# Attention with a gated feed-forward layer: the causal masks of the float32 heads by GpSimd's selection, and the second head's decay row from SBUF on ScalarE's queue

## Chip, cores and metric

One core of a Trainium2 chip runs the whole program. The metric is the device time of one execution in microseconds (us); before the change the median of three runs is 1150.61 us (1149.22 to 1154.78).

The engines are TensorE (PE), VectorE (DVE), ScalarE (ACT), GpSimd (POOL) and SyncE (SP). DMA transfers are issued from the queues of SP, ACT and POOL, which the profile calls SPq, ACTq and POOLq. Each engine works off its own instructions in a fixed order and waits for others by semaphores.

## What is computed

Sixty-four attention heads (8 batches of 8) of 576 rows and 64 columns, with a decay bias made of a running sum, and then a gated layer over the 4608 rows of 512 columns that the heads give:

```python
scores = scale * np.matmul(q, k.transpose(0, 1, 3, 2))
causal = np.triu(np.ones((S, S), dtype=bool), k=1)
cum = np.cumsum(np.maximum(s, 0.0), axis=-1)
bias = -(cum[:, :, :, None] - cum[:, :, None, :])
scores = np.where(causal, -1000000000.0, scores + np.minimum(bias, 0.0))
scores = scores - np.max(scores, axis=-1, keepdims=True)
attn = np.exp(scores)
attn = attn / (np.sum(attn, axis=-1, keepdims=True) + 1e-09)
attn_out = np.matmul(attn, v)
# x: attn_out as 4608 rows of 512
gate = 1.0 / (1.0 + np.exp(-(x @ w_gate)))
out = (gate * (x @ w_val)) @ w_out
```

## The kernel before

**Heads and tiles.** The heads run one after another. Each head is cut into five tiles of query rows, taken from the largest (tile 4, 576 key columns) to the smallest (tile 0, 64 columns). Three kinds of heads follow each other. The first eight, the float32 heads (the first batch, `i < NN` in the code), keep q and k in float32, because the scales with which the others are split into float16 pairs are not there yet. Heads 9 to 16 (the second batch, `NN <= i < MK`) use float16 pairs. So do the rest.

**A float32 head.** `n_prep` (L599) turns q and k of two heads by PE (L614), and ACT copies them to SBUF (L618 to L621, the last being the key copy). `n_s` (L625) makes the scores of one tile in PSUM: one or two float32 products (L631), and then, for the block on the diagonal, one more product by `mask_scores` (L514, the product is L518) that adds 1e30 above the diagonal: a bfloat16 unit matrix `eye` times a constant matrix `above`. `n_max` (L635) is one DVE instruction (L643) that adds the head's decay row to the scores, writes them to SBUF and keeps each row's minimum (scores are held with their sign turned); its second part reads the minimum out. ACT takes the exponential (L644). `n_turn` (L646) turns the result by PE (L653) and ACT (L654), and `n_av` (L656) multiplies it by v (L662).

**The decay row.** `rel` (L166) holds the decay of all heads, one head in each partition. It is written to `cum_d` in HBM (L167). `load_crow` (L444) brings the row of head `i` from there into partition 0 of the tile `cr`, from SP's queue (L447); the first head needs no load, since its row is already in partition 0 of `rel`. `spread_crow` (L449) copies that row to all 128 partitions by POOL (L451). There are two `cr` tiles, so the load for head `i + 2` waits until head `i` no longer reads its tile. Float32 heads read `cr` itself (`bias_row`, L495); later ones read a scaled copy `rl`.

**Masks of the later heads.** In the second batch `s_part` (L481) adds the same bfloat16 product (L518) to its two float16 products (L489, L491). From head 17 on, `mask_part` (L507) does without it: POOL's `affine_select` (L511) writes 1e30 into the columns above the diagonal of `rl`, tile by tile, before `max_part` (L520, DVE L529) adds that row.

**Beside the heads.** During the first heads the kernel also loads the weights of the gated layer, decodes them from 64-bit numbers (ACT L298, DVE L299 to L301), takes a bound for each (PE L310, DVE L313) and splits them into float16 pairs (ACT L337, DVE L338). Their loads are on SP's queue for the first two (L284) and on ACT's queue for the others (L286). Squares of v are loaded from POOL's queue (L184). Each finished batch feeds the gated layer: PE products L714, tanh on ACT (L719), DVE L721, ACT L729 and DVE L730, and the output products L744.

**What sets the order.** The code is written tick by tick, one tile of one head each (L799). A scheduler then lays out each engine's instructions by its own estimate of durations; `tc.high_priority` (the helper `first`) raises the float32 heads in it. A change anywhere in the first heads so moves instructions of other kinds as well. DMA transfers share a small set of completion semaphores (named DMAHW0 to DMAHW7 in the order for the queues of SP and ACT): a transfer that takes a semaphore waits on its own queue until the earlier transfer with that semaphore has landed.

## Time and profile before

| | |
|---|---|
| median of three runs | 1150.61 us |
| the profiled execution, its own time | 1150.28 us |
| its span in the profile | 1148.5 us |
| PE busy | 1096.8 us (96%) |
| DVE busy | 756.4 us (66%) |
| ACT busy | 733.5 us (64%) |
| POOL busy | 199.9 us (17%) |
| first tile of head 2, start of DVE's L643 | 23.46 us |
| first tile of head 3 | 37.24 us |
| first tile of head 9 (DVE's L529) | 97.94 us |

The profile shows one execution. Start times are counted from the start of the span. A busy time is the time in which an engine had at least one instruction under way; products on PE overlap, so the recorded length of one is longer than the step from one to the next. In a row, a bracket names how long the engine had been idle before the instruction and what ended that time. The times of POOL are rough. A share of 96% on PE is a mean over the program: most of what is missing lies in its first fifth.

### The profile page before, as it was taken

How to read it: one execution, taken by the hardware profiler on the slowest of the kernel's cores; microseconds unless marked ns; L12 is line 12 of the kernel's file. 1: busy time of each engine (PE TensorE's matmuls, PEld its weight loads, DVE VectorE, ACT ScalarE, POOL GpSimd, SP SyncE). 2: the span in 40 equal slices, each digit the busy share in tenths (PEclk: the TensorE clock that was granted, in tenths of full speed). 3: DMA queues.
4: the chain of work that ended last, by engine and by line, in shares of the span. 5: the costliest groups of instructions: out<-in, count | busy, mean ns of one | idle time of the engine just before them, and what ended most of it. 6: DMA issues, size and time to landing. Idle time of an engine off the chain costs nothing.

```text
span 1148.5 us, 30266 instructions
## 1 busy us (share of the span) xinstructions
PE 1096.8 (96%) x11868; PEld 861.6 (75%) x11868; DVE 756.4 (66%) x2212; ACT 733.5 (64%) x1437; POOL 199.9 (17%) x473
## 2 busy tenths in 40 slices
PE   6998878999999999999999999999999999999998
PEld 4776757757777887788777777778877787787775
DVE  6868989876787777665565667777777775222222
ACT  5869667867776777676665667778676765233222
POOL 3301101022232222121211122212221211000000
PEclk9999999999999999999999999999999999999999
DMA  9766986997989688866645488878787774000000
GB/s 282 218 189 140 181 178 144 174 200 154 178 159 187 150 186 158 154 139 135 148 87 130 90 175 163 170 144 175 152 159 146 142 123 88 13 20 20 1 19 19
DMA packets 445517, 157.63 MB, mean 137 GB/s; under 512 B 403583, under 2 KB 435839, under 8 KB 445374
## 3 DMA queue, kind: packets, MB, share of 16 engines
q1 hardware_dynamic: 418686, 127.38, 56.7%
q10 hardware_dynamic: 23328, 17.04, 4.9%
q0 software_dynamic: 3360, 11.27, 2.8%
q8 instruction: 93, 1.52, 0.6%
q14 instruction: 50, 0.41, 0.1%
HBM read 56.92 MB, written 9.58 MB: 58 GB/s over the span
## 4 chain that ended last, share of the span: by engine, by line
PE 72%; DMA 10%; DVE 6%; issue 5%; ACT 3%; SPq 3%; POOL 1%; ACTq 0%; DVEq 0%; POOLq 0%
PE gv L714 39%; PE o L744 21%; DMA v<-in_v_dram 3%; PE s L491 3%; PE s L489 2%; DMA T<-qk 2%; PE na_ps L662 1%; SPq L463 1%; DVE e L529 1%; PE av L564 1%; PE av L562 1%; PE av L563 1%; DMA qk<-in_q_dram 1%; DMA w2all<-in_moe_w_out_dram 1%; PE s L631 1%
## 5 line engine op out<-in xcount | busy, mean ns | idle before, releaser
L714 PE MATMUL gv<-x,w 128*128 128x256 f16 (+3 forms) x6912 | 619.2, 247 | 10.1 <-DVE t2f L721 9.1
L714 PEld LDWEIGHTS <-w 128*128 128x128 f16 x6912 | 536.0, 98 | 75.0 <-issue 11.5
L744 PE MATMUL o<-w2all,h 128*128 128x512 f16 x1296 | 313.7, 379 | 1.8 <-ACT h L729 1.8
L530 ACT ACTIVATE e<-e,em 128x576 f32<-128x576 f32 x280 | 153.2, 556 | 92.5 <-DVE em L529 89.8
L744 PEld LDWEIGHTS <-h 128*128 128x128 f16 x1296 | 123.3, 98 | 109.1 <-ACT h L729 2.1
L719 ACT ACTIVATE th<-gv,scb 128x256 f32<-128x256 f32 (+3 forms) x288 | 110.8, 410 | 138.6 <-PE gv L714 130.5
L721 DVE SCALAR_TENSOR_TENSOR t<-th,gv 128x256 f32<-128x256 f32 x192 | 80.0, 417 | 147.9 <-ACT th L719 146.8
L511 POOL TENSOR_SCALAR_AFFINE_SELECT rl<-rl 128x128 f32<-128x128 f32 (+1 forms) x240 | 85.8, 358 | 503.1 <-DVE em L529 462.3
L529 DVE CUSTOM_DVE_ANT_0 e<-s,rl,qkcf 128x576 f32<-128x576 f32 x280 | 151.5, 545 | 31.7 <-PE s L491 15.6
L729 ACT ACTIVATE h<-t,hsc 128x256 f16<-128x256 f32 x192 | 96.7, 504 | 92.4 <-DVE t L721 92.4
L539 DVE SCALAR_TENSOR_TENSOR p<-e,p 128x384 f16<-128x384 f32 x224 | 103.1, 500 | 45.1 <-ACT p L534 44.3
L730 DVE SCALAR_TENSOR_TENSOR h<-t,hsc,h 128x256 f16<-128x256 f32 x192 | 93.7, 488 | 44.9 <-ACT h L729 42.6
L534 ACT ACTIVATE p<-e 128x1152 f16<-128x1152 f32 x112 | 111.9, 1000 | 2.7
L489 PE MATMUL s<-T 128*128 128x288 f16 (+2 forms) x246 | 64.1, 278 | 7.8 <-DVE em L529 4.0
L562 PE MATMUL av<-v,pt 128*128 128x65 f16 x560 | 67.7, 193 | 2.2 <-DMA pt<-p 2.2
L451 POOL PARTITION_BROADCAST cr<-cr x63 | 59.4, 947 | 56.0 <-DMA cr<-cum_d 42.0
L563 PE MATMUL av<-v,pt 128*128 128x64 f16 x560 | 67.7, 192 | 0.0
L564 PE MATMUL av<-v,pt 128*128 128x65 f16 x560 | 67.6, 194 | 0.0
L491 PE MATMUL s<-T 128*128 128x288 f16 (+2 forms) x246 | 61.5, 277 | 4.0 <-DMA T<-T 3.9
L562 PEld LDWEIGHTS <-pt 128*128 128x128 f16 x560 | 52.5, 97 | 7.9 <-DMA pt<-p 3.1
L563 PEld LDWEIGHTS <-pt 128*128 128x128 f16 x560 | 52.5, 97 | 4.5
L564 PEld LDWEIGHTS <-pt 128*128 128x128 f16 x560 | 52.7, 97 | 0.2
(164 smaller groups left out, 1297.0 us busy)
## 6 DMA issues: line engine op xcount, KB each, us to landing
v<-v SPq DMA_DIRECT2D x56, 162.5 KB
out_dram<-io POOLq DMA_DIRECT2D x34, 256.0 KB, 3.2
v<-in_v_dram SPq DMA_DIRECT2D x64, 128.0 KB
T<-T SPq DMA_DIRECT2D x82, 72.0 KB
t2f<-in_v_dram SPq DMA_DIRECT2D x20, 288.0 KB
qk<-in_q_dram SPq DMA_DIRECT2D x17, 288.0 KB
qk<-in_k_dram SPq DMA_DIRECT2D x17, 288.0 KB
w2all<-in_moe_w_gate_dram ACTq DMA_DIRECT2D x7, 512.0 KB
```

Source lines behind the costliest of these rows:

```text
L491: nc.tensor.matmul(ps[:, : b_ - a], lhs, T[i][:, 2, a:b_], start=False, stop=not mask)
L529: nc.vector.tensor_tensor_reduce(e, ps, r, c, MASKED, ALU.add, ALU.min, acc)
L530: nc.scalar.activation(e_t[t][:, :w], e_t[t][:, :w], AF.Exp, bias=acc, scale=-1.0)
L534: nc.scalar.activation(p_s[h_][:, 0], e_s[h_], AF.Copy, scale=PSCALE)
L539: nc.vector.scalar_tensor_tensor(flat[:, LOW[t] * P : (LOW[t] + t) * P], e_t[t][:, : t * P], PSCALE, flat[:, kb * P : (kb + t) * P], ALU.m ...
L562: nc.tensor.matmul(AV[i][:, t], hi, v_[:, D : 2 * D + 1], start=kb == 0, stop=False)
L563: nc.tensor.matmul(AV[i][:, t, 0:D], hi, v_[:, 0:D], start=False, stop=False)
L564: nc.tensor.matmul(AV[i][:, t], lo, v_[:, D : 2 * D + 1], start=False, stop=False)
L714: nc.tensor.matmul(ps[:, gv, a:e], w1[f][:, cc, gv, wl], x_of(b, cc)[:, xl, c0 + a : c0 + e], start=(c == 0), stop=(c == 3 * NC - 1))
L719: nc.scalar.activation(th[:, a:e], ps[:, 0, a:e], AF.Tanh, scale=scb[b][:, f : f + 1])
L729: nc.scalar.activation(h[:, 0], t2, AF.Copy, scale=hsc[:, f : f + 1])
L744: nc.tensor.matmul(ps[:m], h[:, hl, tt * P : tt * P + m], w2[f][:, wl], start=(f == 0 and c == 0), stop=(f == NF - 1 and c == 2))
```

## The change

Three things are changed, and the second batch keeps the bfloat16 product that it has.

- The float32 heads no longer call `mask_scores`. Instead `mask_part` has POOL select in their decay row `cr` itself, tile by tile, as the later heads have it done in `rl`. Tile `t` is selected only after DVE has read the row for the tile before it, since the same columns still counted there.
- The second head's row is no longer read back from HBM on SP's queue, but copied from partition 1 of `rel` to partition 0 of its `cr` tile by a DMA on ACT's queue. `tc.issue_after` places it behind the key copy of the first two heads, the last one noted in `kcopy`.
- `mask_scores` is now called for the second batch alone, and its start column is simplified.

```diff
 def load_crow(i):
     crow[i] = wp.tile([P, S], F32, tag="cr", name=f"cr{i}")
-    if i > 0:
+    if i == 1:
+        with tc.issue_after(kcopy[-1].ins):
+            nc.scalar.dma_start(crow[i][0:1], rel[1:2])
+    elif i > 1:
         nc.sync.dma_start(crow[i][0:1], cum_d[i : i + 1, :])
...
-            mask = i < MK and b_ == w
+            mask = NN <= i < MK and b_ == w
...
 def mask_part(i, t):
-    if i >= MK:
+    if i < NN or i >= MK:
         q0, m, w = TILES[t]
         nc.gpsimd.affine_select(rl[i][:, q0:w], rl[i][:, q0:w], pattern=[[-1, m]], compare_op=ALU.is_ge,
-                                fill=MASKED, base=m - P, channel_multiplier=1)
+                                fill=MASKED, base=0 if i < NN else m - P, channel_multiplier=1)
 def mask_scores(i, t, ps, a):
     q0, m, w = TILES[t]
-    c0 = 0 if i < NN else P - m
-    nc.tensor.matmul(ps[:, q0 - a : w - a], eye, above[:, c0 : c0 + m], start=False, stop=True)
+    nc.tensor.matmul(ps[:, q0 - a : w - a], eye, above[:, P - m :], start=False, stop=True)
...
-                    nc.scalar.copy(kt[:, cols], ps[:, :w])
+                    kcopy.append(nc.scalar.copy(kt[:, cols], ps[:, :w]))
...
-            nc.tensor.matmul(ps[:, : b_ - a], qT[i][:, q0 : q0 + P], kT[p][:, a:b_], start=True, stop=b_ < w)
-            if b_ == w:
-                mask_scores(i, t, ps, a)
+            nc.tensor.matmul(ps[:, : b_ - a], qT[i][:, q0 : q0 + P], kT[p][:, a:b_], start=True, stop=True)
```

Three places show how the instructions move. In the changed program the lines of `load_crow` to `mask_part` stand three further down: the broadcast is L454, the selection L514, the memset of v L462 to L464; those of `n_prep` stand two further down.

POOL at the start, before the change, from the first head's broadcast to behind the second head's (`cr_157` is the first head's row, `cr_196` the second's, `vsq` a load of v to be squared, `nq` a q tile of the third head that is set to zero):

```order
L451 ISA cr_157<-rel 128x576
L184 DMA vsq_0_263<-in_v_dram 128x576
L184 DMA vsq_1_277<-in_v_dram 128x576
L608 MEMSET nq_0_634 64x576
L184 DMA vsq_2_295<-in_v_dram 128x576
L451 ISA cr_196<-cr_196 128x576
L184 DMA vsq_3_319<-in_v_dram 128x576
```

The same place on POOL after the change, where the second head's row is `cr_195`:

```order
L454 ISA cr_157<-rel 128x576
L462 MEMSET v_1_257 64x130
L184 DMA vsq_0_264<-in_v_dram 128x576
L464 MEMSET v_0_159 128x10
L514 AFFINE_SELECT cr_157<-cr_157 128x128
L464 MEMSET v_1_257 128x10
L514 AFFINE_SELECT cr_157<-cr_157 128x128 x2
L610 MEMSET nq_0_667 64x576
L514 AFFINE_SELECT cr_157<-cr_157 128x128
L454 ISA cr_195<-cr_195 128x576
L184 DMA vsq_1_280<-in_v_dram 128x576
L514 AFFINE_SELECT cr_195<-cr_195 128x128
```

The second head's broadcast now stands behind four of the first head's five selections and ahead of two of the loads that it stood behind.

ACT around the first key copies, before the change, with the semaphores that each instruction waits for (`nk` is the turned k of the first two heads, `wa` and `ws` the first weight, `e_80` the scores of the large tiles):

```order
L621 COPY nk_167<-nq_ps_1_0_182 128x288 [waits PE_49]
L621 COPY nk_167<-nq_ps_1_1_187 128x288 [waits PE_49]
L298 ACTIVATE wa_147<-ws_146 128x1024 [waits DMAHW6_49,DMAHW5_49]
L644 ACTIVATE e_80<-e_80,em_4_248 128x576 [waits DVE_49]
L298 ACTIVATE w2all<-w2all 128x1024 [waits DMAHW7_49,DMAHW1_49]
L644 ACTIVATE e_80<-e_80,em_3_274 128x448 [waits DVE_49]
```

The same on ACT after the change:

```order
L623 COPY nk_167<-nq_ps_1_0_182 128x288 [waits PE_49]
L623 COPY nk_167<-nq_ps_1_1_187 128x288 [waits PE_49]
L448 DMA cr_195<-rel 1x16x36 [waits DMAHW5_49,DVE_49]
L298 ACTIVATE wa_147<-ws_146 128x1024 [waits DMAHW6_49]
L644 ACTIVATE e_80<-e_80,em_4_249 128x576 [waits DVE_49]
L644 ACTIVATE e_80<-e_80,em_3_277 128x448 [waits DVE_49]
L298 ACTIVATE w2all<-w2all 128x1024 [waits DMAHW7_49,DMAHW1_49]
```

The load of the second head's row waits for the semaphore of one half of the first weight (DMAHW5), for which the decode behind it waited before; the second decode has moved behind the exponential of the second tile.

DVE at the second head, before the change, from the split of the first weight on (`em_4` and `em_3` are the row minima of tiles 4 and 3, each followed by its read-out, which has one column):

```order
L338 SCALAR_TENSOR_TENSOR w_0_66<-wa_147,wscale,w_0_66 128x8x128
L334 TENSOR_SCALAR wscale<-xe_w_228 128x1
L643 ISA e_80,em_4_353<-s_4_322,cr_196 128x576
L643 ISA em_4_353 128x1
L643 ISA e_80,em_3_364<-s_3_345,cr_196 128x448
L643 ISA em_3_364 128x1
L338 SCALAR_TENSOR_TENSOR w_1_67<-w2all,wscale,w_1_67 128x8x128
```

The same on DVE after the change, down to the third tile:

```order
L338 SCALAR_TENSOR_TENSOR w_0_66<-wa_147,wscale,w_0_66 128x8x128
L643 ISA e_80,em_4_364<-s_4_329,cr_195 128x576
L643 ISA em_4_364 128x1
L313 TENSOR_SCALAR wj_238,wtot_237<-wps_228 128x128
L332 TENSOR_SCALAR xe_w_227<-wtot_237 128x1
L643 ISA e_80,em_3_377<-s_3_354,cr_195 128x448
L643 ISA em_3_377 128x1
L334 TENSOR_SCALAR wscale<-xe_w_227 128x1
L643 ISA e_79,em_2_432<-s_2_367,cr_195 128x320
```

The split of the first weight still stands ahead of the head's first tile; the bound of the second weight has moved in between its tiles, and the split of the second weight behind them.

More of the change, by code (lines that the diff above doesn't have):

```diff
@@ L379, in ffn_scale @@
             out_scale(b)
-    spreads = []
+    spreads, kcopy = [], []
     qk32, qkc, T, crow, v32, v16, vx, PT, xq, rl, AV = {}, {}, {}, {}, {}, {}, {}, {}, {}, {}, {}
```

## The prediction

> **What bounds the kernel now.** I read the page's 40 slices first, to see where TensorE (PE) is not full, then busy times by stretch (columns: stretch in us, length, busy us and instructions of PE, weight loads, VectorE (DVE), ScalarE (ACT) and GpSimd (POOL), granted clock, DMA share, GB/s).
>
> ```profile
> span 1148.5 us, 30266 instructions
> PE   6998878999999999999999999999999999999998
> DVE  6868989876787777665565667777777775222222
> 0.00:106.00 106.00, 89.63 (x661) 73.80 (x662) 74.26 (x213) 80.21 (x162) 26.58 (x62) 0.97 0.78 215
> 106.00:200.00 94.00, 72.96 (x797) 60.69 (x795) 88.45 (x238) 66.69 (x108) 10.40 (x12) 0.95 0.80 162
> 200.00:1148.50 948.50, 934.25 (x10417) 727.09 (x10414) 593.66 (x1763) 586.56 (x1168) 162.94 (x399) 1.00 0.62 126
> ```
>
> From 200 us on PE is busy 934.25 of 948.50 us: that part has its length whatever happens elsewhere, and only starts earlier or later. PE's idle time lies ahead of it: 106.00 - 89.63 = 16.4 us in the first stretch, 94.00 - 72.96 = 21.0 us in the second, where DVE is the full engine (88.45 of 94.00). The change touches the float32 heads, which lie in the first stretch. So the question is by how many microseconds those heads end earlier or later, and whether the DVE-bound stretch passes that on. Within the first stretch:
>
> ```profile
> 20.00:25.00 5.00, 3.29 (x31) 2.97 (x29) 2.78 (x8) 2.49 (x5) 0.86 (x1) 1.00 1.04 331
> 25.00:30.00 5.00, 3.85 (x15) 3.27 (x16) 1.63 (x3) 4.78 (x9) 0.55 (x1) 0.56 1.03 334
> 37.00:98.00 61.00, 55.13 (x427) 45.57 (x426) 43.66 (x135) 49.32 (x105) 11.88 (x22) 1.00 0.70 202
> ```
>
> Around 20 to 30 us every engine waits: DVE is idle for 2.22 + 3.37 = 5.6 us, PE runs at a granted clock of 0.56 in the second half, and the DMA engines are full (share 1.04 and 1.03). This is where the second head begins. From 37 to 98 us (heads three to eight) PE is busy 90% of the time, DVE 72%.
>
> **The change part by part.**
>
> *Masks off PE.* Forty products (eight heads by five tiles) go. The first two rows are the groups of the first 112 us, which hold these forty and ten of the ninth and tenth heads (count, then busy us and mean ns, then idle us); the other three are PE in order of time (start, length).
>
> ```profile
> L518 PE MATMUL s<-above,eye 128*128 128x128 bf16 x40 | 8.8, 228 | 0.0
> L518 PE MATMUL s<-above,eye 128*128 128x64 bf16 x10 | 2.0, 199 | 0.0
> 65.77 0.65 PE L631 MATMUL s<-nk,nq 128*128 128x288 f32 x2
> 66.25 0.22 PE L518 MATMUL s<-above,eye 128*128 128x128 bf16 x1
> 66.31 0.59 PE L631 MATMUL s<-nk,nq 128*128 128x448 f32 x1
> ```
>
> The recorded 228 ns is latency: the next product starts 0.06 us after the mask. So the price of one is between 0.06 us (40 x 0.06 = 2.4 us) and its record (40 x 0.228 = 9.1 us). I take the start-to-start figure, since a pipelined engine is charged by it, and with PE 90% busy in these heads some 2.2 us of it count. If PE is not what is waited for, it is nothing.
>
> *The second head's row.* SyncE's queue (SPq) reaches this load behind the other loads; the broadcast waits for it, and DVE for the broadcast:
>
> ```profile
> 18.47 0.49 SPq L447 DMA_DIRECT2D cr<-cum_d  x1
> 22.57 0.86 POOL L451 PARTITION_BROADCAST cr<-cr  x1 [4.57 <-DMA cr<-cum_d]
> 22.00 0.15 DVE L334 TENSOR_SCALAR wscale<-xe_w 128x1 int32<-128x1 int32 x1
> 23.46 0.76 DVE L643 CUSTOM_DVE_ANT_0 e<-s,cr 128x576 f32<-128x576 f32 x1 [1.32 <-POOL cr L451]
> 8.31 0.40 ACT L621 COPY nk<-nq_ps 128x288 f32<-128x288 f32 x1 [0.41 <-PE nq_ps L614]
> 10.57 1.13 ACT L298 ACTIVATE wa<-ws 128x1024 f32<-128x1024 f32 x1 [1.85 <-DMA ws<-in_moe_w_val_dram]
> 16.70 0.45 ACTq L286 DMA_DIRECT2D ws<-in_moe_w_gate_dram  x1
> ```
>
> In the new order the load stands on ACT's queue between the key copy (ends 8.71) and the first decode (10.57), and waits there for a DMA semaphore that a weight load held before it. The decode behind it waits for that weight load too, so the wait is covered by ACT's 1.85 us of idle time; only the issue itself (0.45 us for such a one) could push the decode, the exponentials and the copies behind it, which the gap hides as well, unless the weight load lands last. The load took 22.57 - 18.47 = 4.1 us from issue; issued at about 10.5 it has landed by 14.6, eight microseconds sooner. DVE does not get eight: its order still has a weight split (L338) ahead of this head's first tile, and that one began at
>
> ```profile
> 20.79 1.28 DVE L338 SCALAR_TENSOR_TENSOR w<-wa,wscale,w 128x1024 f16<-128x1024 f32 x1 [0.68 <-ACT w L337]
> ```
>
> and ended at 22.07, so the sure gain is the wait of 1.32 us. The most is the 5.6 us that DVE idles from 20 to 30. Next late is ACT, which holds the split's other half and the new head's exponentials: 4.78 of 5.00 us busy from 25 on. I take 2.0 us, near the lower end.
>
> *Masks onto POOL.* Forty selections of about 0.36 us (below, 85.8 / 240) are 14 us on an engine with 106.00 - 26.58 = 79 us free there, so its time costs nothing. The order is the cost. Within a head the selection of a tile overwrites columns that the tile before still read, so four selections of five wait for DVE's L643, and the next L643 waits for the selection: a round trip DVE to POOL to DVE that did not exist. Queued behind a waiting L643 is whatever DVE has next (the decode and split of weights, the row sums), and ACT's exponentials and PE's transposes wait for it. On POOL the selections queue behind broadcasts that wait for row loads (4.57 us above). The trace shows the same round trip in the later heads (first row: group on the page; second: waits, total us, times, longest):
>
> ```profile
> L511 POOL TENSOR_SCALAR_AFFINE_SELECT rl<-rl 128x128 f32<-128x128 f32 (+1 forms) x240 | 85.8, 358 | 503.1 <-DVE em L529 462.3
> DVE e L529 <- POOL rl L511: 11.2, 36, 0.6
> 298.78 0.08 DVE L529 DVE_READ_ACCUMULATOR2_ANT em<- 128x1 f32 x1
> 298.94 0.47 POOL L511 TENSOR_SCALAR_AFFINE_SELECT rl<-rl 128x128 f32<-128x128 f32 x1 [8.23 <-DVE em L529]
> 299.45 0.68 DVE L529 CUSTOM_DVE_ANT_0 e<-s,rl,qkcf 128x448 f32<-128x448 f32 x1
> ```
>
> Lower end: as in those heads, 11.2 / 240 = 0.047 us each, 40 x 0.047 = 1.9 us. Upper end: every one of the 32 round trips in full, 299.45 - 298.86 = 0.59 us from accumulator read to next tile, 18.9 us. In the new order of DVE 22 of the 32 have half a microsecond or more of other work between the tiles (mostly a weight step); 10 have less, three of them in the second head: 10 x 0.59 = 5.9 us of waits. DVE has 28% to spare from 37 us on, so I let half of that count: 2.9 us.
>
> How long a selection takes beside DVE's work has a row of its own:
>
> ```profile
> 304.15 0.61 DVE L429 SCALAR_TENSOR_TENSOR qk<-t2f,qksc,qk 96x384 f16<-96x384 f32 x1
> 304.68 0.61 DVE L431 SCALAR_TENSOR_TENSOR qk<-t2f,qksc,qk 96x384 f16<-96x384 f32 x1
> 305.21 0.64 DVE L431 SCALAR_TENSOR_TENSOR t2f<-t2f,qksc 96x384 f16<-96x384 f32 x1
> 304.30 1.14 POOL L511 TENSOR_SCALAR_AFFINE_SELECT rl<-rl 128x128 f32<-128x128 f32 x1 [3.12 <-DVE em L529]
> ```
>
> The same selection that takes 0.47 us at 298.94 took 1.14 us under these three. The Trainium skill, SBUF — State Buffer, section "Who interferes with whom", says that a VectorE instruction with two SBUF inputs and a GpSimd instruction that reads SBUF exclude each other for a whole instruction; by that rule, with which these rows agree, a selection behind a weight step starts only when the step ends and work between the tiles covers nothing: by it this term would be 18.9 us rather than 2.9, and the sum +14.7 us.
>
> *What is only moved.* The instruction order changes on all engines to about 270 us. Those moves have no row. I bound them at a fifth of the second stretch's idle PE time either way, 21.0 / 5 = 4 us, an estimate, and take nothing.
>
> *Sum.* -2.2 - 2.0 + 2.9 = -1.3 us, against the profiled execution: its own time was 1150.28 us, 1.8 us around the span, 0.3 us under the median of 1150.61, too little to matter here. DVE is busy 94% of the next stretch, so what reaches it early is begun early and the gain is passed on: 1149.0 us.
>
> **The rivals.** About 0.5% (5.8 us) is what a measurement of this kernel can tell from no change, so faster means under 1144.9 us and slower over 1156.4 us.
>
> *The start closes up.* The stall from 20 to 30 us goes as a whole: 5.6 us of DVE, with PE at full clock. For it: all engines are idle there at once, and in the new order the third head's query load no longer stands behind the fourth head's row on SPq. Against: the DMA engines are full there with weights. Time: 1150.3 - 2.2 - 5.6 + 1.9 = 1144.4 with the selections at their lower end; if the masks cost PE their recorded 9.1 us, 1137.5.
>
> *The selections become the bound (slower).* Every L643 but a head's first waits its 0.59 us, and DVE's queue with it. It decides from 4.2 us of such waits on the path, where both gains are spent, and can be measured from about 10. Full price: 1150.3 - 4.2 + 18.9 = 1165.0; with three quarters of the 18.9 us on the path 1160.3, with PE's 90% as cover more likely half, 1155.6. For it: the 1.14 us selection above, if weight steps do the same to those beside them. Against: 36 waits in 240 in the later heads. The rule of the Trainium skill named above would bring this rival about.
>
> *Given back.* The float32 heads end earlier, but the next thing is a load that comes no sooner, or the row on ACT's queue lands no earlier because its semaphore comes late (the change would then not do what it says): 1150.3, no change.
>
> **How the numbers follow.** The forecast has 0.42, the closed start 0.25, the selections 0.15, given back 0.18. The closed start reaches from 1137.5 to some 1146; 0.20 of it lie under 1144.9, and 0.05 of the forecast with the 4 us of reordering: faster 0.25. Of the selections 0.10, and 0.03 of the rest with that reordering: slower 0.13. That leaves 0.62 for no change. For the range I leave out about a tenth on each side: at the fast end the closed start with 3 us of good order (1141), at the slow end the selections at half price (1156).
>
> **What would show it.** In the changed profile: no mask product ahead of about 98 us; the row's load on ACT's queue before 11 us and its broadcast before 18; L643's first tile of the second head at about 22.1 instead of 23.46; waits of L643 for the selection of 2 to 6 us in all; and this, the first tile of the third and of the ninth head, 1 to 2 us earlier:
>
> ```profile
> 37.24 0.75 DVE L643 CUSTOM_DVE_ANT_0 e<-s,cr 128x576 f32<-128x576 f32 x1
> 97.94 0.82 DVE L529 CUSTOM_DVE_ANT_0 e<-s,rl,qkcf 128x576 f32<-128x576 f32 x1 [0.71 <-PE s L518]
> ```
>
> A total of more than 10 us in those waits, or a second head that begins before 20 us, would make the forecast wrong, and so would a changed idle time of PE between 106 and 270 us.

## The result, and the profile after

The changed kernel takes 1154.57 us (median of 22 runs, 1149.91 to 1161.44) where the kernel before takes 1150.59 us beside it (22 runs, 1147.42 to 1156.40): the ratio is 1.0032, with a 95% interval of 1.0019 to 1.0045, 3.7 us slower. On two other chips the ratio came out at 1.0009 (0.9978 to 1.0041) and 1.0020 (1.0006 to 1.0034). That is within the 0.5% that the forecast called no change, and inside its range; but the forecast was 1149.0, a gain of 1.3 us. The sign is the other one, and the whole interval on this chip lies above 1.

The profiled execution is the fastest of the 22 (1149.91 us, span 1148.1), so it shows where work moved better than it shows the loss. Slices and stretches of the changed kernel, the same as were shown of before (columns: stretch, length, busy us of PE, weight loads, DVE, ACT, POOL, granted clock, DMA share, GB/s):

```profile
span 1148.1 us, 30291 instructions
PE   7896887999999999999999999999999999999998
DVE  6778998965787778766565577777777775222222
0.00:106.00 106.00, 88.23 (x642) 72.73 (x642) 78.55 (x222) 82.75 (x163) 48.08 (x103) 0.98 0.77 217
106.00:200.00 94.00, 70.70 (x761) 59.10 (x762) 87.27 (x234) 66.91 (x109) 7.31 (x11) 0.91 0.83 166
200.00:1148.10 948.10, 935.83 (x10427) 728.53 (x10424) 594.15 (x1758) 587.09 (x1167) 164.88 (x399) 1.00 0.63 126
20.00:25.00 5.00, 4.85 (x35) 3.83 (x34) 4.05 (x16) 4.07 (x8) 1.63 (x5) 1.00 1.08 356
25.00:30.00 5.00, 3.25 (x25) 2.82 (x26) 2.83 (x6) 4.98 (x13) 1.73 (x3) 1.00 1.12 337
37.00:98.00 61.00, 52.51 (x388) 44.11 (x388) 42.86 (x136) 48.56 (x101) 25.58 (x49) 0.97 0.66 187
```

The stall at 20 to 30 us is partly filled: PE 8.10 us busy of 10 for 7.14 before, DVE 6.88 for 4.41. Behind it nothing is left of that: from 37 to 98 us PE is busy 52.51 of 61 us (55.13 before), and from 106 to 200 us it idles 94.00 - 70.70 = 23.3 us (21.0 before) at a granted clock of 0.91 (0.95). Over the longer stretch of 106 to 270 us, which the prediction had named, PE idles 26.7 us against 25.3; a second profile of the kernel before (e1 below) has 25.8, so this is no clear change. GpSimd went from 26.58 to 48.08 us busy ahead of 106, nearly all of it the 40 selections, which were put at 14 us (group of the line ahead of 106 us: busy time and mean ns of one, then the idle time ahead of them and what ended it):

```profile
L514 POOL TENSOR_SCALAR_AFFINE_SELECT cr<-cr 128x128 f32<-128x128 f32 (+1 forms) x40 | 20.9, 527 | 25.6 <-DVE em L643 22.6 <-DVE wscale L334 0.7 <-DVE qke L411 0.7
```

Single rows in order of time: the row's load on ScalarE's queue, its broadcast, the first tile of the second and of the third head, the first mask product that is left, the first tile of the ninth head.

```profile
8.60 0.66 ACTq L448 DMA_DIRECT2D cr<-rel  x1
15.82 1.28 POOL L454 PARTITION_BROADCAST cr<-cr  x1
20.90 0.74 DVE L643 CUSTOM_DVE_ANT_0 e<-s,cr 128x576 f32<-128x576 f32 x1
31.96 0.75 DVE L643 CUSTOM_DVE_ANT_0 e<-s,cr 128x576 f32<-128x576 f32 x1
97.63 0.22 PE L520 MATMUL s<-above,eye 128*128 128x128 bf16 x1
98.46 0.81 DVE L531 CUSTOM_DVE_ANT_0 e<-s,rl,qkcf 128x576 f32<-128x576 f32 x1
```

The change does what it says. The second head begins 2.6 us earlier than the 23.46 of before, the third 5.3 us earlier than 37.24, and the ninth 0.5 us later than 97.94. So the gain is there at 32 us and gone by 98. These are the waits of L643 for selections in the first 106 us (total, times, longest; the second row is the wait for the first selection, put down to the memset that stands just ahead of it on GpSimd):

```profile
DVE e L643 <- POOL cr L514: 3.8, 10, 0.8
DVE e L643 <- POOL v L464: 3.5, 1, 3.5
```

The ten waits, 3.8 us together, are of the forecast's size. The 3.5 us of the first tile would take the sum to 7.3, but they delay nothing against before: that tile starts at 10.18 us, and in the kernel before at 10.58, where it waits for PE. Ten waits of 3.8 us cannot by themselves eat a lead of 5.3 us and leave a loss.

### The profile page after: what moved, and what is told of

Its sections match the earlier page's. It is cut to its first block, busy times and chain, and to the rows that moved or that the text cites. A ratio compares the mean times of both kernels' runs of the same rounds, so it can differ in the third digit from the quotient of the medians.

```text
span 1148.1 us, 30291 instructions
## 1 busy us (share of the span) xinstructions
PE 1094.8 (95%) x11828; PEld 860.4 (75%) x11828; DVE 760.0 (66%) x2212; ACT 736.7 (64%) x1437; POOL 220.3 (19%) x513
## 4 chain that ended last, share of the span: by engine, by line
PE 73%; DMA 8%; DVE 7%; issue 5%; ACT 3%; SPq 1%; POOL 1%; ACTq 0%; DVEq 0%; POOLq 0%
PE gv L714 40%; PE o L744 21%; PE s L492 3%; PE s L494 2%; DMA T<-qk 1%; DVE e L531 1%; DMA T<-T 1%; PE av L566 1%; PE av L564 1%; PE av L565 1%; DMA v<-in_v_dram 1%; PE s L633 1%; PE na_ps L662 1%; DMA pt<-p 1%; DMA vsq<-in_v_dram 1%
## 5 line engine op out<-in xcount | busy, mean ns | idle before, releaser
L514 POOL TENSOR_SCALAR_AFFINE_SELECT rl<-rl 128x128 f32<-128x128 f32 (+1 forms) x240 | 86.8, 362 | 502.7 <-DVE em L531 465.1
L541 DVE SCALAR_TENSOR_TENSOR p<-e,p 128x384 f16<-128x384 f32 x224 | 101.5, 493 | 44.9 <-ACT p L536 44.0
L454 POOL PARTITION_BROADCAST cr<-cr x63 | 57.3, 912 | 73.8 <-DMA cr<-cum_d 67.0
```

What stands on the lines that cost most here:

```text
L541: nc.vector.scalar_tensor_tensor(flat[:, LOW[t] * P : (LOW[t] + t) * P], e_t[t][:, : t * P], PSCALE, flat[:, kb * P : (kb + t) * P], ALU.m ...
```

## The experiments

Four theories, named in the expectations by letter. **A**: TensorE is starved more often between 98 and 200 us and loses time at half clock. **B**: the round trips DVE to GpSimd to DVE of the selections cost it. **C**: not the new work costs it but the order that the scheduler then gives to everything else. **D**: selections and VectorE's instructions shut each other out at the memory. All ratios are to runs of the kernel before on the same chip. The ninth head's start is from one profile of each run; two profiles of the same program differ in it by 2 us and more (e7 and e15, e1 and the 97.94 of before).

| run | work | order | ratio (95%) | mean clock | ninth head, us |
|---|---|---|---|---|---|
| e1 | before | before | 1.0010 (0.9981 to 1.0039) | 0.9908 | 100.45 |
| e2 | changed | changed | 1.0009 (0.9978 to 1.0041) | 0.9854 | 100.41 |
| e8 | changed | changed | 1.0020 (1.0006 to 1.0034) | 0.9846 | 102.14 |
| e3 | row | its own | 1.0043 (1.0010 to 1.0076) | 0.9835 | 107.71 |
| e4 | selections | its own | 1.0017 (0.9993 to 1.0040) | 0.9878 | 96.34 |
| e5 | changed | before | 1.0043 (1.0024 to 1.0063) | 0.9879 | 103.59 |
| e6 | before | changed | 1.0096 (1.0073 to 1.0118) | 0.9828 | 104.01 |
| e7 | row | before | 0.9985 (0.9968 to 1.0003) | 0.9913 | 96.31 |
| e15 | row | before | 0.9990 (0.9972 to 1.0009) | 0.9913 | 98.45 |
| e9 | row, idle selections in bursts | before | 1.0079 (1.0050 to 1.0109) | 0.9853 | 102.06 |
| e13 | row, idle selections spread | before | 1.0083 (1.0054 to 1.0112) | 0.9870 | 102.84 |
| e17 | the same, reading a constant | before | 1.0027 (1.0014 to 1.0040) | 0.9904 | 99.93 |
| e18 | the same, 4 columns of the row | before | 1.0058 (1.0041 to 1.0075) | 0.9885 | 101.18 |
| e10 | row, first tile's selection | before | 0.9973 (0.9955 to 0.9992) | 0.9906 | 96.91 |
| e16 | row, first tile's selection | before | 0.9988 (0.9971 to 1.0005) | 0.9898 | 99.40 |
| e11 | row, no masks | before | 1.0016 (0.9993 to 1.0038) | 0.9854 | 99.18 |
| e14 | row, no masks | before | 0.9999 (0.9981 to 1.0017) | 0.9865 | 99.52 |
| e12 | changed, each selection twice | changed | 1.0074 (1.0049 to 1.0099) | 0.9826 | 105.47 |

### Both kernels once more

No edit.

> The kernel before, unchanged, for its spread and the granted clock of each of its runs. Theory A (the change starves TensorE between 98 and 200 us more often, so that it loses more time at half clock): these runs have a mean clock of 0.992, a third of the lost time of the changed kernel's 0.9845, and a median near 1150.6. Theory B (the waits for the selections in the first 98 us cost the 4 us, the clock has nothing to do with it): the clock of these runs is the same 0.985 as that of the changed kernel's.

> The changed kernel once more, for a second profiled execution, since the first was the fastest of 22 runs. Theory A: ratio 1.003; if this profile falls near the median of 1154.6, TensorE has two or three more stretches at half clock ahead of 260 us than the six of the first profile, and the head starts fall behind there, not ahead of 98 us. Theory B: the waits of L643 for the selection are longer than the 3.8 us of the first profile, and the ninth head starts some 4 us later than 98.46.

> The changed kernel again, on the chip of these runs, for comparison: ratio 1.001 to 1.004 and clock 0.985 by either theory.

Measured: the kernel before has a mean clock of 0.9908 over 12 runs, and of 0.9895 to 0.9913 in the comparison runs of the five chips; the changed kernel 0.9845, 0.9854 and 0.9846 over 22, 12 and 12. So theory A's sign is there every time: by these clocks (1 - 0.985) x 1152 = 17 us count as lost, against 11, an estimate. Theory B's sign is not: the waits for selections in e2's profile come to 3.1 us and in e8's to 4.1, about the 3.8 of the first. Within the 22 runs of the changed kernel time and clock go together (6.5 us for 0.01 of clock, correlation -0.67). But one profile of the kernel before (span 1156.5) has its 23rd head at 331.35 us, another at 325.55: two profiles of one kernel differ more than the two kernels do, and single profiles prove nothing here. A says which kernel is starved, not by what. Nor does the mean clock decide the time: of the runs below, e9 and e11 have 0.9853 and 0.9854 on one chip and are 7 us apart, and e17 is 3 us slower than the kernel before at 0.9904, where that has 0.9913.

### One part alone

```diff
 e3: before, and
+        if i == 1:
+            with tc.issue_after(kcopy[-1].ins):
+                nc.scalar.dma_start(crow[i][0:1], rel[1:2])
...
 e4: before, and
-            mask = i < MK and b_ == w
+            mask = NN <= i < MK and b_ == w
...
-        if i >= MK:
+        if i < NN or i >= MK:
```

> The kernel before with only the second head's row on ScalarE's queue; the masks stay products. Theory B: no selections, so same or faster than before, ratio 0.998 to 1.000, second head's first tile near 21 us. Theory C (what counts is the order that the scheduler makes behind about 98 us, which any edit at the start changes): the second head starts early as well, but the gain is gone by the tenth head, and the ratio can be anything from 0.996 to 1.005, with no relation to the masks.

> The kernel before with only the selections for the first eight heads; the second head's row stays on SyncE's queue. Theory B: slower, ratio 1.003 to 1.006, with the second head at 23.5 us and the loss there ahead of 98 us. Theory C: the ninth head starts within 2 us of the kernel before's 97.94, and the ratio can be anything from 0.996 to 1.005 by what happens behind it.

Measured: neither part is a gain alone. The selections alone come to 1.0017, under the 1.003 that B asked for, with the ninth head at 96.34 us, within the 2 us that C allowed. The row by itself is the worse of the two, 1.0043. In its profile the second head begins at 19.69 us, 3.8 us before the kernel before, and the third at 39.60, 2.4 us behind it. PE and DVE there (a helper's three extra lines shift the numbers: L634 is the score product, L665 the value product, L646 the first pass over a tile):

```profile
33.29 3.52 PE L665 MATMUL na_ps<-v,p 128*128 128x65 f32 x16
36.60 2.76 PE L634 MATMUL s<-nk,nq 128*128 128x288 f32 x4
39.60 0.76 DVE L646 CUSTOM_DVE_ANT_0 e<-s,cr 128x576 f32<-128x576 f32 x1 [3.65 <-PE s L521]
```

```profile
32.00:36.00 4.00, 4.00 (x19) 3.71 (x18) 2.71 (x3) 3.22 (x6) 1.39 (x2) 0.50 0.88 241
36.00:40.00 4.00, 4.00 (x13) 2.71 (x13) 0.40 (x1) 0.00 (x0) 0.00 (x0) 0.50 0.64 220
```

Sixteen value products now stand between the halves of the third head's scores, PE runs at a clock of 0.50, DVE waits 3.65 us, and ACT does nothing from 36 to 40. These rows show the row's load nowhere; what differs there is the order. B falls for this run, and C gains.

### The work of one kernel in the order of the other

The program's instructions are the same ones apart from the masks and one load, so a table of the place that each has on its engine can hold them in the other kernel's order, up to about 300 us (2820 rows of PE, 690 of DVE, 500 of ACT, 240 of SP, 155 of POOL). Masks, selections and the row's load are left to the scheduler.

```diff
+ORDER = {
+    "PE": """
...
+        for a, b in zip(place, place[1:]):
+            tc.add_manual_dep(rows[engine][b], rows[engine][a].name, mybir.DependencyInfo(
+                mybir.DependencyClass.NoSync, mybir.DependencyReason.DATA), reason="issue_after")
```

> The changed kernel's work (selections, row on ScalarE's queue), with all other instructions held in the order of the kernel before on every engine up to about 300 us. Theory C (the new order of everything else costs the time, not the new work): ratio to before 0.997 to 1.000, mean granted clock 0.990 as before, ninth head no later than 98 us. Theory B (the selections' waits cost it): ratio 1.003 or more, clock 0.985 or less.

> The work of the kernel before (masks as products, second head's row on SyncE's queue behind the other loads), with all other instructions held in the order of the changed kernel. Theory C: slower than before by as much as the changed kernel or more, ratio 1.002 to 1.008, clock 0.985 or less, since the order goes with the loss and here the row is late as well. Theory B: ratio 0.998 to 1.001, clock 0.990.

> Only the second head's row moved to ScalarE's queue, in the order of the kernel before. Theory C: the loss of the row alone (ratio 1.0043 in its own order) goes, ratio 0.997 to 1.000; the second head starts 1.3 us earlier than before, near 22.1 us, since VectorE's order there is unchanged. Theory B' (the row's issue on ScalarE's queue holds up ScalarE or takes DMA time from the weights): ratio 1.003 or more in this order too, with ScalarE late ahead of 20 us.

Measured: both crossings lose, 1.0043 and 1.0096. So C as it was put (the order alone) falls, and so does B alone. (In e6 the second head's row also comes late for its order, so its 11 us are not the order's alone.) The row by itself, held in the order of before, is 1.0043 no longer but 0.9985, and 0.9990 when run again: the same work, some 6 us apart by its order, on different chips. There the second head starts at 21.19 and the ninth at 96.31 us. Adding the selections in that same order, and taking the 40 products away, costs (1.0043 - 0.9985) x 1152 = 6.7 us, and in these two profiles the ninth head comes 7.3 us later. That is the new work's own price, free of reordering of the other work; the scheduler's own order (1.0020 on this chip) gives 2.6 us of it back. DVE's waits for selections in this run, ahead of 98 us:

```profile
DVE e L731 <- POOL cr L600: 9.9, 18, 1.6
```

18 waits, 9.9 us: this looked like theory B.

### Selections that nobody waits for

```diff
 e9: row on ACT's queue, masks as products, and
+        if i < NN:
+            q0, m, w = TILES[t]
+            nc.gpsimd.affine_select(
+                idle[:, : min(m, 104)], crow[i][:, q0 : q0 + min(m, 104)], pattern=[[-1, min(m, 104)]], ...)
 e13: the same, each at the place on GpSimd that the real one has in e5
 e17: as e13, reading  ident[:, : min(m, 104)]  and not the row
 e18: as e13, with     idle[:, :4], crow[i][:, q0 : q0 + 4]
```

> The row on ScalarE's queue and the masks as products, all in the order of the kernel before (as in the run of the row in that order, ratio 0.9985), and beside them 40 selections on GpSimd that read the rows of the first eight heads, in bursts behind each broadcast, and write a buffer that nobody reads: GpSimd's and VectorE's meeting at the memory, without the round trip. Theory D (selections and VectorE instructions shut each other out, so that selections cost VectorE their time whoever waits): ratio 1.003 to 1.006, VectorE's instructions longer ahead of 98 us. Theory B (the round trip of 9.9 us of waits is what costs): ratio 0.997 to 1.000, as without them.

> The row on ScalarE's queue, masks as products, order of the kernel before, and 40 idle selections (nobody waits for what they write, and they wait for no tile) at the places of GpSimd's order that the real ones have. If the round trip is what the selections cost: ratio 0.998 to 1.001, close to the row alone. If GpSimd's time alone costs it (its later work, on which VectorE and the loads wait): 1.003 to 1.008, as with the bursts.

> As the run with idle selections at the real ones' places, but they read a constant of the same size and not the row: GpSimd's time as there, the row's buffer held no longer than by VectorE. If GpSimd's time costs it: ratio 1.004 to 1.009. If the held row buffer costs it: 0.998 to 1.001, and the third pair's query load issued near 30 us.

> As the run with idle selections at the real ones' places, reading the row, but 4 columns each instead of 64 to 104: the row's buffer is read at the same places, with less of GpSimd's time. If GpSimd's time costs it: ratio 0.999 to 1.003, in proportion to the time left. If the held row buffer costs it: 1.005 or more as there.

Measured: without any round trip the idle selections cost as much as the real ones and more, 1.0079 in bursts and 1.0083 spread. So a cost of this size needs no round trip, and B is not needed to explain it; how much the round trips of the real selections add is not measured by these runs. Theory D, in which VectorE's instructions get longer, does not fit either: in e9's profile its weight steps take 1.23 and 1.22 us and the first pass over a tile 0.75 us, as in e7's. (In e13 some are longer, about 1.7 us in all ahead of 98 us against e15.) What the idle selections do is seen in the bursts' profile. GpSimd from 31 us (L601 the idle selections, L541 a broadcast, L283 the reduction of v's statistic, for which DVE's L285 waits):

```profile
30.98 4.19 POOL L601 TENSOR_SCALAR_AFFINE_SELECT idle<-cr 128x104 f32<-128x104 f32 x5
...
35.72 1.33 POOL L541 PARTITION_BROADCAST cr<-cr  x1
37.12 3.01 POOL L601 TENSOR_SCALAR_AFFINE_SELECT idle<-cr 128x104 f32<-128x104 f32 x5
40.11 0.44 POOL L283 PARTITION_ALL_REDUCE vst<-vss  x1
```

DVE waits for that reduction, and PE for what stands behind it on DVE:

```profile
40.59 0.16 DVE L285 TENSOR_REDUCE vso<-vst 128x1 f32<-128x4 f32 x1 [1.23 <-POOL vst L283]
```

```profile
42.96 2.29 PE L728 MATMUL s<-nk,nq 128*128 128x288 f32 x4 [1.46 <-DVE em L740]
```

The same four products in the run of the row alone (e7):

```profile
39.95 1.24 PE L722 MATMUL s<-nk,nq 128*128 128x288 f32 x4 [0.15 <-DVE em L734]
```

GpSimd is late, DVE waits 1.23 us behind it, PE waits 1.46 us behind DVE, and then its products take 2.29 us for 1.24, at a granted clock of 0.50 (43 to 46 us). In e9 none of these waits bears the name of a selection. Nor do its selections hold a row's buffer: the fourth head's row, which goes into the second head's buffer, is loaded at 30.12 us, right behind VectorE's last read of it, which ends at 30.05, and the later ones up to 91 us follow that read within 0.1 us as well. So in bursts GpSimd's time alone costs about (1.0079 - 0.9987) x 1152 = 11 us over the row alone (the mean of e7 and e15, on other chips; 7 to 14 us by the intervals).

Spread out (e13), a second way shows on SyncE's queue. A row's load there waits until its buffer is free, and the loads of the third pair's q and k stand behind it. With the row alone (e15; the first line of each is two row loads as one group, so its length holds the wait between them):

```profile
17.70 11.60 SPq L536 DMA_DIRECT2D cr<-cum_d  x2
30.03 0.89 SPq L687 DMA_DIRECT2D nqk<-in_q_dram  x2
```

with idle selections spread (e13):

```profile
19.37 14.04 SPq L538 DMA_DIRECT2D cr<-cum_d  x2
33.64 0.88 SPq L694 DMA_DIRECT2D nqk<-in_q_dram  x2
```

reading a constant (e17), and reading 4 columns of the row (e18):

```profile
17.47 12.10 SPq L538 DMA_DIRECT2D cr<-cum_d  x2
30.48 0.92 SPq L694 DMA_DIRECT2D nqk<-in_q_dram  x2
```

```profile
18.02 14.29 SPq L538 DMA_DIRECT2D cr<-cum_d  x2
32.53 0.88 SPq L694 DMA_DIRECT2D nqk<-in_q_dram  x2
```

An idle selection reads the row's buffer, so the buffer is held until GpSimd has come to it: the query load goes out 3.6 us later in e13 and 2.5 us in e18, but 0.5 us in e17. (The other profile of the row alone, e7, has it at 28.41, so profiles of one program differ by 1.6 us here. The hold itself is plainer: from the end of VectorE's last read of the second head's row to the load that refills the buffer it is 2.8 us in e13 and in e18, and 0.1 us in e17.) In e13 ScalarE's next load then starts 2.4 us behind the one before it, and the profile puts the copies' wait behind that down to SyncE's k load; that the two queues shared a semaphore there is inferred (ACT and PE of e13; L752 copies the turned scores out, L751 is the turn):

```profile
40.24 0.44 ACTq L374 DMA_DIRECT2D w2all<-in_moe_w_gate_dram  x1
43.05 0.37 ACTq L374 DMA_DIRECT2D w2all<-in_moe_w_val_dram  x1
43.47 0.86 ACT L752 COPY p<-nt_ps 128x384 f32<-128x384 f32 x2 [4.21 <-DMA nqk<-in_k_dram]
```

```profile
44.00 0.90 PE L751 MATMUL nt_ps<-ident,e 128*128 128x128 f32 x3 [2.92 <-ACT p L752]
```

The two prices come apart in e17: with the buffer held no longer, 40 idle selections cost 1.0027 - 0.9990 = 0.0037 or 4 us (GpSimd's time ahead of its other work; the row alone was on other chips, and by the intervals it is 2 to 7 us); with the buffer held (e18, on e17's chip, and e13) another 0.003 to 0.006, 4 to 6 us. The cut to 4 columns in e18 did not do what it was meant to: its selections keep GpSimd busy for 20.0 us, those of e17 for 21.0. So e18 differs from e17 by the held buffer and hardly by GpSimd's time. For e17 both expectations failed: 1.0027 lies under the 1.004 to 1.009 of GpSimd's time alone and over the 0.998 to 1.001 of the buffer alone. For idle selections spread out it is both.

The held buffer, though, belongs to the idle selections. A real one stands ahead of VectorE's read of the same tile, so VectorE is the last reader. These are VectorE's last read of the second head's row in e5, the row loads (the last of the two, for the fourth head, ends at 18.16 + 13.03 = 31.19) and the query load:

```profile
30.70 0.22 DVE L731 CUSTOM_DVE_ANT_0 e<-s,cr 64x64 f32<-64x64 f32 x1 [0.24 <-POOL cr L600]
18.16 13.03 SPq L536 DMA_DIRECT2D cr<-cum_d  x2
31.38 0.88 SPq L686 DMA_DIRECT2D nqk<-in_q_dram  x2
```

The load goes out as soon as VectorE has read, and VectorE had waited 0.24 us for a selection there, and 1.58 us at the tile before, whose selection stood behind a memset and a broadcast on GpSimd. So what selections add to the delay of that load in e5 is VectorE's wait for them, and no hold of their own. In the changed kernel's own order the query load no longer stands behind the fourth head's row and goes out at 26.80 us, 5.7 us earlier than the 32.52 of before. So of the two prices of idle selections only GpSimd's time can carry over to the changed kernel. Its 4 us in e17 and the 6.7 us of the real selections in e5 are not clearly apart (1.0014 to 1.0040 and 1.0024 to 1.0063); what the 9.9 us of waits add in e5 stays open.

### Masks off TensorE

```diff
 e11, e14: row on ACT's queue, and
-            nc.tensor.matmul(ps[:, : b_ - a], qT[i][:, q0 : q0 + P], kT[p][:, a:b_], start=True, stop=b_ < w)
-            if b_ == w:
-                mask_scores(i, t, ps, a)
+            nc.tensor.matmul(ps[:, : b_ - a], qT[i][:, q0 : q0 + P], kT[p][:, a:b_], start=True, stop=True)
 e10, e16: the product stays for t < NTL - 1; a selection for t == NTL - 1
```

> The row on ScalarE's queue and no mask at all in the first eight heads (neither product nor selection, so these heads see all columns), order of the kernel before: what the 40 products cost TensorE. By the prediction's 0.06 us each: 2.2 us faster than the row alone, ratio 0.996 to 0.997. If TensorE is not what is waited for there: 0.9985 as the row alone. If they cost their recorded 228 ns: 9 us, ratio 0.991.

> As the run without any mask in the first eight heads, beside the row alone on the same chip. If the 40 products cost TensorE 0.06 us each on the path: 2.2 us below the row alone. If TensorE is not waited for there: the same as the row alone. If fewer products let TensorE fall to half clock more often: above the row alone by 2 to 4 us, with a clock lower by 0.004.

> Only the row on ScalarE's queue, order of the kernel before, as the ground for the two runs above: ratio 0.997 to 1.000, clock 0.991.

> The row on ScalarE's queue; only the first tile of each of the first eight heads is masked by a selection (8 of 40, none of which has a tile before it that still reads the columns), the other 32 by products; order of the kernel before. Theory B: no round trip, so ratio 0.996 to 0.999, at or below the row alone. If single selections cost whatever the round trip: a fifth of the selections' 6.7 us, 1.3 us over the row alone, 0.9985 to 1.001.

> The row, and a selection for the first tile alone of the first eight heads, order of the kernel before: ratio 0.996 to 0.999 as on the first chip, clock 0.991; if its gain was the row's alone, equal to the run of the row beside it.

Measured, e14 beside e15 on one chip: mean 1152.0 us (standard error 0.8) without any mask, 1150.5 (0.5) with all 40 products. Taking the products away gains nothing, and not the 2.2 us that were forecast; it is 1.5 us slower if anything, with a mean clock of 0.9865 for 0.9913 (0.9854 for 0.9913 in the first pair, on different chips). So TensorE's products are not what is waited for there. That the lower clock comes of its having less to do, and that it costs the 1.5 us, was not shown, nor is the 1.5 us itself beyond doubt. One selection a head, for the first tile, does no harm: 0.9973 and 0.9988. On the second chip that equals the row alone (0.9990), so its gain is the row's.

### Twice the selections

```diff
 e12: the changed kernel in its own order, and under each selection for i < NN
+                nc.gpsimd.affine_select(rl[i][:, q0:w], rl[i][:, q0:w], pattern=[[-1, m]], ...)
```

> The changed kernel in its own order, with each of the 40 selections of the first eight heads issued twice. The second one adds 0.3 to 1.2 us to each round trip. Theory B: the round trips lie on the path for about a half, so 32 times 0.5 us times a half, 8 us over the changed kernel: ratio 1.007 to 1.012. If the waits were hidden in the changed kernel's own order: 1.002 to 1.004 as without.

Measured: 1.0074, so 40 more selections cost another 5 to 7 us over the changed kernel. Here the waits of DVE grow as well (ahead of 98 us; the second selection is L604):

```profile
DVE e L734 <- POOL cr L604: 14.2, 21, 1.8
DVE e L734 <- POOL cr L600: 1.2, 1, 1.2
```

From 3.8 us in the changed kernel, or 7.3 with its first tile's, to 15.4: the selections are not hidden in the changed kernel's own order either. This run does not tell the round trip from GpSimd's time.

## Why the prediction was wrong

*The second head's row, -2.0.* Right in size. Alone and in the order of before it measured (0.9985 - 1) x 1152 = -1.7 and -1.2 us, though both intervals reach just over 1. The load went out at 8.60 and the broadcast came at 15.82, as forecast (before 11, before 18); the issue on ScalarE's queue was covered, as the first decode starts at 10.11 us for 10.57 before. The first tile at 20.90 is 1.2 us earlier than the 22.1 that was forecast.

*Selections on POOL, +2.9.* **This is the step that failed**, in the sentence "on an engine with 106.00 - 26.58 = 79 us free there, so its time costs nothing. The order is the cost." GpSimd's time was put at nothing. Idle selections that nobody waits for, and that hold no buffer, cost 4 us spread out (e17) and about 11 us in bursts (e9). The time itself was too small as well: 40 selections took 20.9 us and not 14. The waits that the prediction then priced came out as priced in the changed kernel, 3.8 us of the 2 to 6 forecast; held in the order of before they were 9.9 us, and the whole of the selections cost 6.7 us there, with the products gone. The prediction named what queues behind a waiting L643, and did not ask what queues behind a selection on GpSimd (v's reduction, the next broadcast, the loads of v). A mean of free time says nothing of the few places where the next thing is due.

*Masks off PE, -2.2.* Wrong: nothing was gained in e11 and e14. The prediction itself said when it would be nothing ("if PE is not what is waited for") and then let PE's 90% decide. The waits of PE in the kernel before, from 20 to 106 us, say it better:

```profile
PE nq_ps L614 <- ACT nq L619: 2.5, 2, 1.6
PE na_ps L662 <- ACT p L654: 1.5, 2, 1.2
PE nt_ps L653 <- ACT e L644: 1.5, 2, 1.2
```

The three largest are all for ACT, 5.5 us together. That shorter score products do not end them sooner is what e11 and e14 say; the rows by themselves do not.

*What is only moved, 0 within 4 us.* Too narrow. The same work in two orders differs by some 6 us (the row alone: 1.0043 and 0.9985 to 0.9990), and the kernel before in the order of the changed one is 11 us slower. A fifth of the idle time of the next stretch had no ground. The prediction's own signs of being wrong did not show any of this: the waits are under 10 us, the second head begins after 20 us, and PE's idle time from 106 to 270 us is 26.7 us for 25.3.

*Sum.* In the order of before: row -1.7, selections with the masks off PE +6.7, together +5.0 (e5's 1.0043, from which the 6.7 was taken, so that this is no check); the scheduler's own order gives back 2.6 on that chip: +2.3 (1.0020), +3.7 and +1.0 on the others. The lead of the third head, 5.3 us where 1 to 2 were forecast, goes with order too: its query load, which the prediction had seen move forward, goes out 5.7 us earlier. It was lost again by the ninth head. That the measured time lies inside the range is luck: the terms that were forecast do not add up to it.

*The rivals.* "The selections become the bound" had the sign and the price (1155.6 at half). Its waits are there in e5 (9.9 us, half of 18.9) but not in the changed kernel (3.8 us), and a cost as large comes without any of them (e9, e13). The rule of the Trainium skill, SBUF — State Buffer, section "Who interferes with whom" (a VectorE instruction with two SBUF inputs and a GpSimd instruction that reads SBUF exclude each other), is borne out as to the lengthening: a selection takes 0.24 us at the least and 1.2 beside two-input weight steps, as shown below. It did not come to 18.9 us of waits. "Given back" is what the third to ninth heads show. "The start closes up" did not happen as a whole: DVE got 2.5 of the 5.6 us.

*What was shown and what was not.* Shown by runs: the price of the selections in a fixed order, that GpSimd's time alone has a price, what a held buffer costs beside it when the selections are idle ones, the nothing of the masks, and that order is worth 6 us and more. Only seen in single profiles: which instruction waits for which at 36 to 44 us. Open: how much of the real selections' 6.7 us is GpSimd's time and how much the round trip, how much of the changed kernel's 1 to 4 us in its own order is order and how much selections, and how much of any of them the lower clock adds.

The version that came out best is the row alone on ScalarE's queue with everything else held in the order of before (0.9985, 0.9990), with or without the selection of the first tile (0.9973, 0.9988): 1 to 3 us under the kernel before in all four runs, though only the interval of 0.9973 stays under 1.

## What to carry to other kernels

Free time on an engine is not a price of zero: before moving work to it, list what stands behind the new instructions on that engine's queue and when each is due, and, where the new instruction is the last to read a buffer, which load, on which queue, waits for it. Where a scheduler orders the program, measure an edit twice, in its own order and held in the old one; here the same edit, the row alone, read 0.4% slower and 0.1% faster. Taking work off an engine that is itself waiting gained nothing here, at 90% busy.

## What the runs showed of the hardware

A selection's length was hardly a matter of its size. Instructions of 64 to 104 columns (e13) and of 4 columns (e18), duration in ns as least, median and most:

```profile
L602 POOL TENSOR_SCALAR_AFFINE_SELECT idle<-cr x40: 238/278/1224, 9.2 to 97.1; 128x104 f32<-128x104 f32 x32, 128x64 f32<-128x64 f32 x8
```

```profile
L602 POOL TENSOR_SCALAR_AFFINE_SELECT idle<-cr x40: 188/229/1265, 9.2 to 95.8; 128x4 f32<-128x4 f32 x40
```

A cut to 4 columns takes 0.05 us off the least and nothing off the most. The longest go with VectorE's work: three selections and DVE beside them in e13.

```profile
31.09 3.35 POOL L602 TENSOR_SCALAR_AFFINE_SELECT idle<-cr 128x104 f32<-128x104 f32 x3
```

```profile
31.82 1.23 DVE L388 SCALAR_TENSOR_TENSOR wa<-wa,w 128x1024 int32<-128x1024 int32 x1
33.09 1.22 DVE L389 SCALAR_TENSOR_TENSOR wa<-ws,wa 128x1024 int32<-128x1024 int32 x1
```

The second and third selection, 2.46 us from 31.98 us on, last as long as the two weight steps, which keep their own 1.22 us. (VectorE is not always spared: its next step of this kind, at 35.58 us, takes 1.62.) So selections beside two-input VectorE work are better priced at VectorE's pace than at their own: 20.9 us for 40 in the changed kernel, and not 40 x 0.295 = 11.8 by their median of 0.295 there.

Some stalls of TensorE went with a stretch at half clock: after the 2.92 us of waiting in e13 the granted clock was 0.62 over the next 4 us, and after the 1.46 us in e9 0.50 from 43 to 46 us.

```profile
44.00:48.00 4.00, 4.00 (x14) 2.78 (x14) 1.26 (x5) 4.00 (x11) 1.13 (x3) 0.62 1.11 318
```

In slices of 1 us the stretches at 0.50 come in multiples of some 3.4 us: ahead of 200 us in the profile of the kernel before from about 26 to 33, 111 to 118 and 165 to 168 us, in that of the changed one from about 50 to 54, 108 to 118, 153 to 156 and 180 to 183 us. That is five and six times 3.4 us, an estimate of 1.7 us lost each time if PE has work throughout. The Trainium skill, TensorE: Matmul & The Clock Gate, section "HAM oscillation — how this bites in real kernels", says that a wait that crosses the monitor's window makes the next work start at half rate; these rows agree as to the half rate, though the waits in its example are over 3.4 us long and those here were 2.92 and 1.46.
